# Layer one's last pair with seven partial second products, and some low parts on VectorE

## The chip, the cores and the metric

The kernel runs on one core of one Trainium2 chip. The metric is the device time of one execution in microseconds (us); the value before is 744.51, the median of three runs (744.11 to 745.92). The engines are TensorE (PE, with its weight loads PEld), VectorE (DVE), ScalarE (ACT), GpSimd (POOL) and SyncE (SP), which issues the transfers. Each engine does its own instructions in order.

## What is computed

An attention over clusters, whose result x has 1536 rows and 512 columns, is followed by two feed-forward layers. The change lies in the first of them and in the step to the second.

```python
x = attention(q, k, v, centroids)            # 1536 x 512
h = x @ moe_w_in                             # 512 -> 2048
x = np.maximum(0.01 * h, h) @ moe_w_out      # layer one
h = x @ moe2_w_in
r = np.maximum(h, 0.0)
return (r * r) @ moe2_w_out                  # layer two
```

All operands are float32. A float32 product is made of three matmuls in a shorter format: each operand is split into a high part (a cast) and a low part (operand minus its high part), and high by high, high by low and low by high are added up in PSUM.

## The kernel before

Layer m has the 1536 rows in three blocks b of 512 rows, and the 2048 inner columns in eight pairs f = 0, 2, ..., 14 of two 128-wide slices f and f + 1. For every pair the first product gives h, the activation gives g, and the second product adds to `acc[:, b, o]`, with o the four 128-column parts of the output. Blocks 0 and 1 of a pair form a two by two product. With seven first products in place of eight (Winograd's scheme), `quad` and `seven` compute P1 to P7; each is 2 x 3 matmuls of 512 columns. The inputs of these products are differences t1 to t4 of parts of x (`t_ops`; high parts `th`, low parts `tl`) and sums of the weights (`sum_pieces`, tile `ws`; block (m, f, 2)).

In layer one, pairs 4 to 12 (`SEVEN`) go through `seven`, which also does the second product of blocks 0 and 1 with seven products, M1 to M7, of six matmuls each, and needs one more sum of weights, block (0, f, 3), whose four additions GpSimd does in the pair before. Block 2 has plain products: u0 and u1 (12 matmuls each) and o0 to o3 (6 each). Such a pair has 132 matmuls. Pair 14, the last of layer one, goes through `step_list` and `quad`: eight second products, 138 matmuls, and block 2's second product at its very end.

The order on TensorE, VectorE, ScalarE and GpSimd is the program's own from pair 2 on (`manual_schedule`). Inside `seven` it is a string of names (`SEVEN_QUAD`): P1 is that product's matmuls, k1, k5 and k6 are ScalarE's copies of a bank to `q`, aV, aX and aW are VectorE's sums in the four banks U, V, W and X, B11 to B22 the activated blocks with h, f and l for the high part, the full value and the low part, T1 to T4 their differences, r1.0 the addition of a half of M1's bank to `acc`, f0 the same for o0. n0.2 is step 2 of block 0 of the pair after: step 0 loads the raw weights, 1 does the first arithmetic (ScalarE and GpSimd), 2 joins both halves (VectorE), 3 casts the high part `wh` (ScalarE), 4 subtracts the low part `wl` (GpSimd). c is the pair's own blocks (c3.1 is the high part of the sum block, c3.2 its low part) and l the pair after the next.

When the last addition of layer one to `acc` is made, `flush` also writes the next layer's x: high part `xh` by ScalarE, low part `xl`. For blocks 0 and 1 GpSimd does the low part, from `acc`; for block 2 VectorE adds into the PSUM bank itself and does the four low parts from that bank, after all four additions:

```python
x, eng = (ps, nc.vector) if b == 2 else (a, nc.gpsimd)
nc.vector.tensor_tensor(out=x, in0=ps, in1=a, op=ALU.add)
nc.scalar.copy(out=xh[:, o, c], in_=x)
```

Layer two's pair 0 is plain: units (0, 0), (0, 1) and (1, 0) of 12 matmuls, each followed by a maximum with zero on ScalarE, a square on VectorE, a cast to `gh` on ScalarE and a low part `gl` on VectorE; then the second product of unit (0, 0). The eight differences for layer two (`SUMS[1]`, L1285 in the rows) are GpSimd's, from `acc`.

Of the kernel before, what the change touches and what calls it, by code (L numbers as in the profile page):

```python
# [74 lines left out]
    "n1.2 g11 B22h B22f T3 T2 T1h T2h T1l T4 u0 T2l u0h u0f u0l T3h T3l n1.3 n1.4 "  # L75
) + SEVEN_REST + " h4.0 h4.1"
DOTS = {(0, 0): 0, (0, 1): 1, (1, 0): 2}


@with_exitstack  # L80
def attention_moe_moe_kernel(
# [25 lines left out]
    RING = 7  # L107
    SEVEN = (4, 6, 8, 10, 12)
    SIDE = 4
# [52 lines left out]
    def split_block(ci, t):  # L162
        pool = next(q for q, n in ring if ci % RING < n)
        wh = pool.tile([128, 2 * DM], F32R, tag="wh", name="wh")
        wl = pool.tile([128, 2 * DM], F32R, tag="wl", name="wl")
        weights[blocks[ci]] = (wh, wl)
        nc.scalar.copy(out=wh, in_=t)  # L167
        return lambda: nc.gpsimd.tensor_tensor(  # L168
            out=wl, in0=t, in1=wh.bitcast(F32), op=ALU.subtract
        )  # L170

    def decode_pieces(ci):
# [40 lines left out]

        def rest():
            st["rest"]()

# [10 lines left out]
    def sum_pieces(ci):  # L227

        st = {}
        K = DM // 2  # L230

        def sums():
            w = st["w"] = stg[1].tile([128, 4, K], F32, tag="ws", name="ws")
            m, f, j = blocks[ci]
            t0, t1 = (words[blocks.index((m, f, i))] for i in range(2))
            if j == 2:
                a11, a12, a21, a22 = t0[:, 0:K], t0[:, K : 2 * K], t1[:, 0:K], t1[:, K : 2 * K]
            else:
                a11, a12, a21, a22 = (
                    t[:, DM + i * K : DM + (i + 1) * K] for i in range(2) for t in (t0, t1)  # L240
                )
            for o, i, k, op in (
                (w[:, 0], a21, a22, ALU.add),
                (w[:, 1], w[:, 0], a11, ALU.subtract),
                (w[:, 2], a11, a21, ALU.subtract),
                (w[:, 3], a12, w[:, 1], ALU.subtract),
            ):
                nc.gpsimd.tensor_tensor(out=o, in0=i, in1=k, op=op)

        def high():  # L250
            st["rest"] = split_block(ci, st["w"].rearrange("p a b -> p (a b)"))

        return [sums, high, lambda: st["rest"]()]

# [766 lines left out]

    x_low = []

    def flush(m, b, g, o, ps, part=slice(0, 512)):
        a = acc[:, b, o, part]
        if g == 0:
            nc.scalar.copy(out=a, in_=ps)
            return
        if g < NF // 2 - 1:
            nc.vector.tensor_tensor(out=a, in0=ps, in1=a, op=ALU.add)  # L1030
            return
        if m == 0:
            c = slice(b * N, (b + 1) * N)
            x, eng = (ps, nc.vector) if b == 2 else (a, nc.gpsimd)
            nc.vector.tensor_tensor(out=x, in0=ps, in1=a, op=ALU.add)
            nc.scalar.copy(out=xh[:, o, c], in_=x)
            if b == 2:
                x_low.append((o, c, x))
                if o < 3:
                    return  # L1040
                todo = list(x_low)
                x_low.clear()
            else:
                todo = [(o, c, x)]
            for o, c, x in todo:
                eng.tensor_tensor(
                    out=xl[:, o, c], in0=x, in1=xh[:, o, c].bitcast(F32), op=ALU.subtract
                )
# [6 lines left out]
    def quad(m, f, behind=True):  # L1055
        f0, f1, s = ((m, f, j) for j in range(3))
# [10 lines left out]
        def first():  # L1067
            p(U, lambda k: w_in(f0, k), lambda k: x_in(k, 0), True)
            p1 = tmp()
            nc.scalar.copy(out=p1, in_=U)  # L1070
            p(V, lambda k: w_in(f0, 2 + k), lambda k: x_in(2 + k, 0), True)
            add(V, V, p1)
            if behind:
                act(m, 0, f, V)

        kept = []

        def second():
# [36 lines left out]
    def seven(f, prev, after, later):  # L1115
# [119 lines left out]
        for name, q, block, c, g, b, half in (  # L1235
# [19 lines left out]
        for o in range(4):  # L1255
            ops[f"o{o}"] = lambda o=o: last(o)
            ops[f"f{o}"] = lambda o=o: flush(0, 2, f // 2, o, st["o", o])
        for i, q in enumerate(prev):
            ops[f"bh{i}"] = lambda q=q: g2(*q)
        for c, base in (("n", after), ("l", later), ("c", (0, f))):  # L1260
            for k in range(4):
                for j in range(5):
                    ops[f"{c}{k}.{j}"] = lambda base=base, k=k, j=j: piece((*base, k), j)
        for kk in range(2):
# [68 lines left out]
    def step_list(m, f, prev):  # L1333
# [55 lines left out]

    def piece(block, j):  # L1390
# [5 lines left out]
        pieces[block][j]()  # L1396

# [11 lines left out]
    for m in range(2):  # L1409
        turn = 0  # L1410
        for f in range(0, NF, 2):
# [80 lines left out]
```

## Time and profile before

| what | us |
|---|---|
| median of three runs | 744.51 |
| the profiled execution, its own time | 747.96 |
| its span | 746.20 |
| TensorE busy | 738.1 |
| pair 12 of layer one, TensorE's first matmul to the next pair's first | 429.38 to 459.34 |
| pair 14 of layer one | 459.34 to 491.20 |

The profile is one execution. TensorE hardly stops from one end to the other, so a time is read as a number of matmuls and the waits between them. The other engines have room on average; what counts is which of their instructions TensorE waits for at one place. In a timeline each row has the start, the duration, the engine, the line and operation, and in brackets how long the engine stood still before and what it waited for.

### The profile page before, as it was taken

Reading aid. Unit: us, or ns where it says so; the run is one execution under the profiler, and the core shown is the slowest. Engines: PE = TensorE matmul, PEld = TensorE weight load, DVE = VectorE, ACT = ScalarE, POOL = GpSimd, SP = SyncE. Lnnn points to the kernel's source line nnn. Section 1 sums busy time; section 2 is a strip of 40 time slices with the busy share of each in tenths; the row PEclk is TensorE's granted clock in tenths of the full one; section 3 lists DMA queues with packets and bytes.
Section 4 is the critical chain, followed back from the end, with each engine's and each line's share of the span. In section 5 each row is a group of like instructions: output and inputs, shape, how many; then the busy total and the mean of one; then the engine's idle time right before and its main releaser. Section 6 shows DMA issues by size and latency. Waiting matters only on the chain.

```text
span 746.2 us, 11181 instructions
## 1 busy us (share of the span) xinstructions
PE 738.1 (99%) x4014; PEld 643.1 (86%) x4014; DVE 534.6 (72%) x845; ACT 453.2 (61%) x837; POOL 497.6 (67%) x467
## 2 busy tenths in 40 slices
PE   8999999999999999999999999999999999999998
PEld 7999999999998878888888888788888888888886
DVE  6989999999998535376766866564667666576655
ACT  5988988988999465356365463656644335443430
POOL 7999999999957747866797874599434342343400
PEclk8999999999999999999999999999999999999999
DMA  3494663662612311111121130211212111121004
GB/s 108 123 226 118 134 162 109 133 164 65 152 44 83 122 65 72 57 57 60 63 105 56 58 114 11 102 58 56 76 44 107 57 56 66 54 108 58 1 0 170
DMA packets 16407, 64.79 MB, mean 87 GB/s; under 512 B 3040, under 2 KB 4192, under 8 KB 11360
## 3 DMA queue, kind: packets, MB, share of 16 engines
q1 hardware_dynamic: 16352, 64.07, 28.9%
q8 instruction: 32, 0.52, 0.3%
q14 instruction: 23, 0.19, 0.1%
HBM read 43.02 MB, written 3.15 MB: 62 GB/s over the span
## 4 chain that ended last, share of the span: by engine, by line
PE 91%; ACT 3%; DVE 3%; POOL 2%; issue 1%; DMA 0%; POOLq 0%; DVEq 0%; ACTq 0%
PE h L910 32%; PE o L988 23%; PE A L576 8%; PE S L479 7%; PE T L541 7%; PE o L1217 6%; PE h L1217 4%; PE S L350 1%; ACT e L511 1%; DVE nm L501 1%; PE o L1018 1%; DVE el L558 1%; PE dots L350 1%; POOL xl L606 0%; POOL q L1285 0%
## 5 line engine op out<-in xcount | busy, mean ns | idle before, releaser
L168 POOL TENSOR_TENSOR wl<-wt,wh 128x1024 fp32r<-128x1024 f32 x32 | 77.3, 2416 | 74.4 <-ACT wh L167 73.9
L910 PE MATMUL h<-xh,wh 128*128 128x512 f32 x288 | 112.0, 391 | 0.3 <-DVE h L1063 0.3
L910 PE MATMUL h<-xh,wl 128*128 128x512 f32 x288 | 112.2, 389 | 0.0
L910 PE MATMUL h<-xl,wh 128*128 128x512 f32 x288 | 112.2, 389 | 0.0
L1030 DVE TENSOR_TENSOR acc<-o,acc 128x512 f32<-128x512 f32 x154 | 100.0, 685 | 11.8 <-PE o L988 11.8
L558 DVE TENSOR_TENSOR el<-T,eh 128x512 fp32r<-128x512 f32 x144 | 94.6, 683 | 2.9 <-ACT eh L552 2.2
L528 POOL TENSOR_SCALAR e<-e,r 128x768 f32<-128x768 f32 x96 | 86.4, 911 | 12.7 <-PE T L541 6.8
L501 DVE TENSOR_REDUCE nm<-S 128x1 f32<-128x768 f32 x96 | 90.9, 948 | 3.5 <-PE S L350 1.8
L511 ACT ACTIVATE e<-S,nm 128x768 f32<-128x768 f32 x96 | 87.2, 908 | 10.0 <-DVE ds L378 5.3
L479 PE MATMUL S<-hb 128*128 128x384 f32 x384 | 89.8, 348 | 0.3 <-ACT xt L589 0.2
L552 ACT CAST eh<-T 128x512 fp32r<-128x512 f32 x144 | 79.6, 590 | 8.7 <-PE T L541 8.5
L959 DVE TENSOR_TENSOR gl<-h,gh 128x512 fp32r<-128x512 f32 x66 | 45.0, 691 | 54.0 <-ACT h L954 35.6
L576 PE MATMUL A<-eh,vv 128*128 128x256 f32 x288 | 80.3, 308 | 0.6 <-DVE xt L598 0.6
L541 PE MATMUL T<-ident,e 128*128 128x128 f32 x576 | 79.7, 273 | 0.5 <-POOL e L528 0.5
L576 PE MATMUL A<-el,vv 128*128 128x256 f32 x288 | 73.0, 283 | 0.2 <-DVE el L558 0.2
L541 PEld LDWEIGHTS T<-ident,e 128*128 128x128 f32 x576 | 68.9, 143 | 3.6 <-POOL e L528 0.7
L988 PE MATMUL o<-wh,gh 128*128 128x512 f32 x184 | 71.6, 389 | 0.0
L988 PE MATMUL o<-wl,gh 128*128 128x512 f32 x184 | 71.6, 389 | 0.0
L988 PE MATMUL o<-wh,gl 128*128 128x512 f32 x184 | 71.6, 389 | 0.0
L944 ACT ACTIVATE t<-h 128x512 f32<-128x512 f32 x48 | 28.0, 599 | 71.3 <-PE h L910 38.0
L168 POOL TENSOR_TENSOR wl<-ws,wh 128x1024 fp32r<-128x1024 f32 x17 | 41.4, 2433 | 38.2 <-ACT wh L167 38.2
L910 PEld LDWEIGHTS h<-xh,wh 128*128 128x128 f32 x288 | 54.1, 188 | 12.4 <-DVE gl L1177 0.7
(188 smaller groups left out, 1750.0 us busy)
## 6 DMA issues: line engine op xcount, KB each, us to landing
wraw<-w SPq DMA_DIRECT2D x32, 1024.0 KB, 4.7
hb<-spl SPq DMA_DIRECT2D x14, 576.0 KB, 4.7
hb<-spl SPq DMA_DIRECT2D x42, 192.0 KB, 5.1
rqk<-qk SPq DMA_DIRECT2D x16, 384.0 KB, 3.8
rv<-v SPq DMA_DIRECT2D x8, 384.0 KB, 3.4
out<-q SPq DMA_DIRECT2D x11, 256.0 KB, 2.8
hb<-st SPq DMA_DIRECT2D x56, 24.0 KB, 1.9
out<-q SPq DMA_DIRECT2D x2, 128.0 KB, 1.8
```

Of the source, the lines that this page charges most:

```text
L168: return lambda: nc.gpsimd.tensor_tensor(out=wl, in0=t, in1=wh.bitcast(F32), op=ALU.subtract)
L479: nc.tensor.matmul(out=s[:, c, 0:HALF], lhsT=hb[:, a, i * 128 : (i + 1) * 128], rhs=hb[:, b, c * HALF : (c + 1) * HALF], start=(a == 0), s ...
L501: nc.vector.tensor_reduce(out=n, in_=s_t[t][:, :, 0:HALF], axis=AX.XY, op=ALU.max, negate=True)
L511: nc.scalar.activation(out=e.rearrange("p (a b) -> p a b", a=2), in_=s_t.pop(t)[:, :, 0:HALF], func=AF.Exp, bias=n_t.pop(t), scale=1.0, ac ...
L528: nc.gpsimd.tensor_scalar(out=e_t[t], in0=e_t[t], scalar1=r_t[t // 2][:, t % 2 : t % 2 + 1], scalar2=1.0, op0=ALU.mult, op1=ALU.mult,)
L541: nc.tensor.transpose(T[:, o : o + 128], e_t[2 * u + b][:, kc * 128 : (kc + 1) * 128], ident)
L552: nc.scalar.copy(out=eh[:, 2 * g : 2 * g + 2, :].rearrange("p a b -> p (a b)"), in_=T_t[u, g])
L558: nc.vector.tensor_tensor(out=el[:, 2 * g : 2 * g + 2, :].rearrange("p a b -> p (a b)"), in0=T_t.pop((u, g)), in1=eh[:, 2 * g : 2 * g + 2, ...
L576: nc.tensor.matmul(out=A, lhsT=w, rhs=m[:, kc, :], start=(kc == 0 and i == 0), stop=(kc == KC - 1 and i == 1),)
L910: nc.tensor.matmul(out=out, lhsT=l, rhs=r, start=(first and i == 0), stop=(i == n - 1), skip_group_check=not first,)
L988: nc.tensor.matmul(out=outs[o], lhsT=l, rhs=r, start=(first and i == 0), stop=(last and i == 2),)
L1030: nc.vector.tensor_tensor(out=a, in0=ps, in1=a, op=ALU.add)
```

## The change

Pair 14 also goes through `seven`, with an order of its own, `SEVEN_LAST`. Its four-fold sum of weights, block (0, 14, 3), is new work of GpSimd in pair 12. In that order a D at the end of a name puts a low part on VectorE: c3.2D and n0.4D (`wl`, 128 x 1024 each) and B11lD (128 x 512). `flush` now adds into `acc` for block 2 too, and the low parts of x for block 2 (x2.0 to x2.3) and for the last two column parts of block 0 (x0.2, x0.3) are kept for later and done by VectorE from `acc`. Six differences of layer two (t1, t2, t4) stand in the new order; before they were in `SUMS[1]` under -2 and -1.

```diff
+SEVEN_LAST = (
+    "n0.1 P1 k1 P2 c3.1 c3.2D n0.2 aV n1.0 P6 k6 B11h B11f P5 k5 B11lD n0.3 n0.4D P7 aX B22h B22f P3 "
+    "aW B12f P4 B21h B21f T1 T3 B21l T2 n1.1 T1h T2h T1l n1.2 T4 u0 T2l u0h u0f u0l T3h T3l n1.3 l0.0 "
+    "M1 M2 r1.0 r1.1 n1.4 r2.0 r2.1 B22l u1 u1h u1f u1l M6 M5 r6.0 r5.0 r5.1 r6.1 o0 f0 M3 T4h r3.0 M7 "
+    "r7.0 T4l r7.1 r3.1 o1 f1 M4 r4.0 r4.1 x0.2 x0.3 l0.1 t1.0 t1.1 t2.0 t2.1 t4.0 t4.1 o2 f2 o3 f3 "
+    "x2.0 x2.1 x2.2 x2.3 l0.2 l1.0"
+)
...
-    SEVEN = (4, 6, 8, 10, 12)
+    SEVEN = (4, 6, 8, 10, 12, 14)
...
-        return lambda: nc.gpsimd.tensor_tensor(
+        return lambda eng=nc.gpsimd: eng.tensor_tensor(
             out=wl, in0=t, in1=wh.bitcast(F32), op=ALU.subtract
         )
...
-            x, eng = (ps, nc.vector) if b == 2 else (a, nc.gpsimd)
-            nc.vector.tensor_tensor(out=x, in0=ps, in1=a, op=ALU.add)
-            nc.scalar.copy(out=xh[:, o, c], in_=x)
-            if b == 2:
-                x_low.append((o, c, x))
-                if o < 3:
-                    return
-                todo = list(x_low)
-                x_low.clear()
+            nc.vector.tensor_tensor(out=a, in0=ps, in1=a, op=ALU.add)
+            nc.scalar.copy(out=xh[:, o, c], in_=a)
+
+            def low(eng):
+                eng.tensor_tensor(
+                    out=xl[:, o, c], in0=a, in1=xh[:, o, c].bitcast(F32), op=ALU.subtract
+                )
+
+            if later is not None:
+                later[b, o] = low
             else:
-                todo = [(o, c, x)]
-            for o, c, x in todo:
-                eng.tensor_tensor(
-                    out=xl[:, o, c], in0=x, in1=xh[:, o, c].bitcast(F32), op=ALU.subtract
-                )
+                low(nc.gpsimd)
...
+            ops[n + "lD"] = lambda n=n: low(n, nc.vector)
...
-                ops[f"r{name}.{j}"] = lambda q=q, j=j, b=b, o=2 * half + j: flush(
-                    0, b, f // 2, o, st[q, j]
+                g = f // 2 if f < NF - 2 or name in "2347" else 1
+                ops[f"r{name}.{j}"] = lambda q=q, j=j, b=b, g=g, o=2 * half + j: flush(
+                    0, b, g, o, st[q, j], later=x_low if b == 0 and o > 1 else None
                 )
...
+            for b in (0, 2):
+                ops[f"x{b}.{o}"] = lambda b=b, o=o: x_low[b, o](nc.vector)
...
-        for name in (SEVEN_PLAIN if f < 2 * PLAIN[0] else SEVEN_QUAD).split():
+            for name in ("t1", "t2", "t4"):
+                ops[f"{name}.{kk}"] = t_by[1][kk][name]
+        order = SEVEN_PLAIN if f < 2 * PLAIN[0] else SEVEN_QUAD if f < NF - 2 else SEVEN_LAST
+        for name in order.split():
             ops[name]()
```

VectorE at the start of pair 14, before: after the last addition of pair 12 (`acc<-h`) come the sum in bank V (`h<-h,q`), the join of `wt`, and then low parts and sums.

```order
L1030 TENSOR_TENSOR acc<-h,acc 128x512
L1063 TENSOR_TENSOR h<-h,q 128x512
L206 SCALAR_TENSOR_TENSOR wt<-wt,wraw 128x1024
L959 TENSOR_TENSOR gl<-h,gh 128x512
L1063 TENSOR_TENSOR h<-h,q 128x512 x2
```

The same place now:

```order
L1035 TENSOR_TENSOR acc<-h,acc 128x512
L175 TENSOR_TENSOR wl<-ws,wh 128x1024
L213 SCALAR_TENSOR_TENSOR wt<-wt,wraw 128x1024
L1124 TENSOR_TENSOR h<-h,q 128x512
L1177 TENSOR_TENSOR gl<-t,gh 128x512
L175 TENSOR_TENSOR wl<-wt,wh 128x1024
L1124 TENSOR_TENSOR h<-h,q 128x512 x2
```

A low part of 128 x 1024 (c3.2D) and the join now stand ahead of the sum in V, and a second one (n0.4D) ahead of the sums in X and W.

VectorE at the step from layer one to layer two, before: the join for pair 2 of layer two, the four additions of block 2 and their low parts, and then the square and the low part of layer two's first unit.

```order
L206 SCALAR_TENSOR_TENSOR wt<-wt,wraw 128x1024
L1035 TENSOR_TENSOR o<-o,acc 128x512 x4
L1046 TENSOR_TENSOR xl<-o,xh 128x512 x4
L947 SCALAR_TENSOR_TENSOR h<-h,t 128x512
L959 TENSOR_TENSOR gl<-h,gh 128x512
```

The same place now, from the last additions of M4 (r4.0, r4.1) on:

```order
L1039 TENSOR_TENSOR acc<-o,acc 128x512 x2
L1043 TENSOR_TENSOR xl<-acc,xh 128x512 x2
L1039 TENSOR_TENSOR acc<-h,acc 128x512 x2
L1043 TENSOR_TENSOR xl<-acc,xh 128x512 x4
L213 SCALAR_TENSOR_TENSOR wt<-wt,wraw 128x1024
L954 SCALAR_TENSOR_TENSOR h<-h,t 128x512
L966 TENSOR_TENSOR gl<-h,gh 128x512
```

Six low parts that read `acc` and the join now stand ahead of the square; the four of before read a PSUM bank, and the join stood ahead of the additions.

GpSimd at the same step, now: the low part of layer two's second block, six low parts of x, the first step on the next raw weights, and the differences.

```order
L175 TENSOR_TENSOR wl<-wt,wh 128x1024
L1043 TENSOR_TENSOR xl<-acc,xh 128x512 x6
L207 TENSOR_SCALAR wraw<-wraw 128x1024
L1295 TENSOR_TENSOR q<-acc 128x512 x2
L1295 TENSOR_TENSOR q<-acc,q 128x512 x2
```

Before, it had eight low parts of x, four ahead of that block's low part and four behind the step on the raw weights, and then the same differences.

## Rows read from the trace of the kernel before

**Rows 1.** The page, part 1: busy us (share of the span) xinstructions.

```profile
PE 738.1 (99%) x4014; PEld 643.1 (86%) x4014; DVE 534.6 (72%) x845; ACT 453.2 (61%) x837; POOL 497.6 (67%) x467
```

**Rows 2.** Timeline of TensorE, pairs 12 and 14: start us, us, engine, what, [idle before].

```profile
429.38 0.39 PE L910 MATMUL h<-xh,wh 128*128 128x512 f32 x1
...
459.34 0.39 PE L910 MATMUL h<-xh,wh 128*128 128x512 f32 x1
...
467.28 0.39 PE L910 MATMUL h<-xh,wl 128*128 128x512 f32 x1
467.94 0.50 PE L910 MATMUL h<-xh,wh 128*128 128x512 f32 x1 [0.28 <-DVE h L1063]
...
491.20 0.39 PE L910 MATMUL h<-xh,wh 128*128 128x512 f32 x1
...
499.36 0.39 PE L988 MATMUL o<-wh,gh 128*128 128x512 f32 x1
```

**Rows 3.** Timeline of VectorE, first part of pair 12.

```profile
430.18 1.22 DVE L206 SCALAR_TENSOR_TENSOR wt<-wt,wraw 128x1024 int32<-128x1024 int32 x1
432.37 0.70 DVE L1124 TENSOR_TENSOR h<-h,q 128x512 f32<-128x512 f32 x1 [0.96 <-PE h L910]
436.43 0.70 DVE L1124 TENSOR_TENSOR h<-h,q 128x512 f32<-128x512 f32 x1 [3.37 <-PE h L910]
```

**Rows 4.** Timeline of GpSimd, the same place.

```profile
432.55 2.40 POOL L168 TENSOR_TENSOR wl<-ws,wh 128x1024 fp32r<-128x1024 f32 x1 [2.85 <-ACT wh L167]
```

**Rows 5.** Timeline of ScalarE, the same place.

```profile
431.42 1.05 ACT L167 CAST wh<-ws 128x1024 fp32r<-128x1024 f32 x1
...
434.14 0.60 ACT L1164 ACTIVATE gh<-h 128x512 fp32r<-128x512 f32 x1
...
435.11 0.61 ACT L1136 COPY q<-h 128x512 f32<-128x512 f32 x1
435.57 1.08 ACT L167 CAST wh<-wt 128x1024 fp32r<-128x1024 f32 x1
```

**Rows 6.** Timeline of VectorE and GpSimd, low parts (xl) with both inputs in SBUF.

```profile
340.27 1.29 DVE L1329 TENSOR_TENSOR xl<-t,xh 128x512 fp32r<-128x512 f32 x2
...
518.21 2.40 POOL L168 TENSOR_TENSOR wl<-wt,wh 128x1024 fp32r<-128x1024 f32 x1
...
519.39 1.77 DVE L1329 TENSOR_TENSOR xl<-t,xh 128x512 fp32r<-128x512 f32 x1 [0.78 <-ACT xh L1328]
...
520.57 2.85 POOL L168 TENSOR_TENSOR wl<-ws,wh 128x1024 fp32r<-128x1024 f32 x1
...
521.86 2.11 DVE L1329 TENSOR_TENSOR xl<-t,xh 128x512 fp32r<-128x512 f32 x1 [0.70 <-ACT xh L1328]
```

**Rows 7.** Timeline of VectorE and ScalarE, step to layer two.

```profile
492.00 2.48 DVE L1046 TENSOR_TENSOR xl<-o,xh 128x512 fp32r<-128x512 f32 x4
...
494.75 0.70 DVE L947 SCALAR_TENSOR_TENSOR h<-h,t 128x512 f32<-128x512 f32 x1 [0.26 <-ACT t L944]
...
495.48 0.59 ACT L956 CAST gh<-h 128x512 fp32r<-128x512 f32 x1 [0.77 <-DVE h L947]
```

**Rows 8.** Timeline of GpSimd, step to layer two.

```profile
493.03 2.54 POOL L1285 TENSOR_TENSOR q<-acc 128x512 f32<-128x512 f32 x2
```

**Rows 9.** Timeline of VectorE and GpSimd, around 256 us.

```profile
255.75 1.28 POOL L256 TENSOR_SCALAR xh<-xt 128x768 fp32r<-128x768 f32 x1
...
256.26 1.84 DVE L206 SCALAR_TENSOR_TENSOR wt<-wt,wraw 128x1024 int32<-128x1024 int32 x1
...
257.00 2.26 POOL L1285 TENSOR_TENSOR q<-q 128x512 f32<-128x512 f32 x1
```

**Rows 10.** Busy by stretch: PE PEld DVE ACT POOL busy (x), PEclk, DMA share, GB/s.

```profile
8.00:12.00 4.00, 4.00 (x22) 4.00 (x22) 2.71 (x6) 3.14 (x5) 3.04 (x2) 0.54 0.08 32
12.00:20.00 8.00, 8.00 (x52) 7.30 (x52) 5.69 (x12) 5.02 (x9) 4.75 (x4) 0.80 0.01 2
```

**Rows 11.** Waits of TensorE, the longest: us in total, times, longest.

```profile
PE ctp L312 <- DVE ct L310: 1.5, 1, 1.5
```

More of the change, by code (lines that the diff above doesn't have):

```diff
@@ L212, in high, with rest @@
             st["rest"] = split_block(ci, st["t"].bitcast(F32))
-        def rest():
-            st["rest"]()
+        def rest(*eng):
+            st["rest"](*eng)
         if ci < EARLY:
@@ L251, in high @@
             st["rest"] = split_block(ci, st["w"].rearrange("p a b -> p (a b)"))
-        return [sums, high, lambda: st["rest"]()]
+        return [sums, high, lambda *eng: st["rest"](*eng)]
     def pool_copy(out, in_):
@@ L1020, in last_rows, with flush @@
                 flush(1, b, NF // 2 - 1, o, ps, c)
-    x_low = []
-    def flush(m, b, g, o, ps, part=slice(0, 512)):
+    def flush(m, b, g, o, ps, part=slice(0, 512), later=None):
         a = acc[:, b, o, part]
@@ L1053, in flush, with quad @@
             nc.sync.dma_start(out=out[r : r + 128, part], in_=ob)
-    def quad(m, f, behind=True):
+    def quad(m, f):
         f0, f1, s = ((m, f, j) for j in range(3))
@@ L1072, in first @@
             add(V, V, p1)
-            if behind:
-                act(m, 0, f, V)
+            act(m, 0, f, V)
         kept = []
@@ L1082, in second @@
                 nc.scalar.copy(out=kept[-1], in_=q)
-            if not behind:
-                act(m, 0, f, V)
         def third():
@@ L1121, in seven @@
         ops = {}
+        x_low = {}
         def add(out, a, b, op=ALU.add):
@@ L1256, in seven @@
             ops[f"o{o}"] = lambda o=o: last(o)
-            ops[f"f{o}"] = lambda o=o: flush(0, 2, f // 2, o, st["o", o])
+            ops[f"f{o}"] = lambda o=o: flush(0, 2, f // 2, o, st["o", o], later=x_low)
+            for b in (0, 2):
+                ops[f"x{b}.{o}"] = lambda b=b, o=o: x_low[b, o](nc.vector)
         for i, q in enumerate(prev):
@@ L1263, in seven @@
                     ops[f"{c}{k}.{j}"] = lambda base=base, k=k, j=j: piece((*base, k), j)
+                    ops[f"{c}{k}.{j}D"] = lambda base=base, k=k, j=j: piece(
+                        (*base, k), j, nc.vector
+                    )
         for kk in range(2):
             ops[f"h4.{kk}"] = t_by[0][kk]["h4"]
-        for name in (SEVEN_PLAIN if f < 2 * PLAIN[0] else SEVEN_QUAD).split():
+            for name in ("t1", "t2", "t4"):
+                ops[f"{name}.{kk}"] = t_by[1][kk][name]
+        order = SEVEN_PLAIN if f < 2 * PLAIN[0] else SEVEN_QUAD if f < NF - 2 else SEVEN_LAST
+        for name in order.split():
             ops[name]()
@@ L1350, in step_list @@
             return seq, tail
-        first, second, third = quad(m, f, bool(behind))
-        behind = behind or [lambda: None] * 2
+        first, second, third = quad(m, f)
         seq = [
@@ L1358, in step_list @@
         if f == NF - 2:
-            if m == 1:
-                return seq + [lambda: last_rows(2)], []
-            return seq + [lambda: g2(*tail[0]), lambda: g2(*tail[1])], []
+            return seq + [lambda: last_rows(2)], []
         return seq, tail
@@ L1382, in attention_moe_moe_kernel @@
         {
-            -2: "t1.0 t1.1 t2.0 t2.1", -1: "t4.0 t4.1", 0: "t3.0 t3.1", 2: "h1.0 h1.1 l1.0 l1.1",
+            0: "t3.0 t3.1", 2: "h1.0 h1.1 l1.0 l1.1",
             3: "h2.0 h2.1", 4: "l2.0 l2.1", 5: "h3.0 l3.0", 6: "h3.1 l3.1", 8: "h4.0", 9: "h4.1",
@@ L1388, in attention_moe_moe_kernel, with piece @@
     pieces = {}
-    def piece(block, j):
+    def piece(block, j, *eng):
         if block not in blocks:
@@ L1395, in piece @@
             pieces[block] = (sum_pieces if block[2] > 1 else decode_pieces)(i)
-        pieces[block][j]()
+        pieces[block][j](*eng)
     def pair_after(m, f):
@@ L1435, in attention_moe_moe_kernel @@
                     piece((0, 2, 0), 0)
-                table = {(0, NF - 2): TURN_LAST, (1, 0): TURN_SEAM}.get((m, f), TURN)
+                table = TURN if (m, f) != (1, 0) else TURN_SEAM
                 for k, j in table[i] if i < len(table) else ():
@@ L1441, in attention_moe_moe_kernel @@
                 sums(m, turn)
-                if m == 0 and f == NF - 2:
-                    sums(1, i - len(seq))
                 turn += 1
```

3 lines of the change are left out of this document (removed).

## Prediction

> **What bounds the kernel now.** I read the page's busy shares first: TensorE is busy 99% of the span [rows 1]. So only two things can move the time: fewer matmuls, or a wait of TensorE. Next came TensorE's own timeline around the last pair of layer one [rows 2]. A 512-wide matmul starts every 0.2267 us (36 of them from 491.20 to 499.36: 8.16 / 36). The pair before the last, with 132 matmuls, runs from 429.38 to 459.34: 29.96 us against 132 x 0.2267 = 29.92. The last pair, with 138 matmuls in the plain order, runs from 459.34 to 491.20: 31.86 against 138 x 0.2267 = 31.28, so it loses 0.58; the largest piece is the gap in front of 467.94, where TensorE waits for VectorE (467.28 + 0.2267 = 467.51, so 0.43). Then I laid the other three engines beside it, since the change gives VectorE work that GpSimd had.
>
> **What the change takes away.** Six matmuls: 6 x 0.2267 = 1.36 us. With the new order the old gap has no place either, so the most that can be won is 31.86 - 29.92 = 1.94 us, 0.26% of 744.51. About 0.3% (2.2 us) is what a measurement of this kernel can tell from no change, so even the full gain would hardly show.
>
> **The start of the last pair.** I use the pair from 429.38 as the template, since the first seven products keep its order, and count from its first matmul as 0. P1, P2, P6, P5, P7, P3 and P4 then start at 0, 1.36, 2.72, 4.08, 5.44, 6.80 and 8.16. In the template VectorE does the join of wt at 0.80 and the sum aV at 2.99, as soon as P2 ends [rows 3], and the low part of the sum block (c3.2) runs on GpSimd for 2.40 [rows 4]. In the new order c3.2D stands on VectorE ahead of that join and of aV. It must wait for ScalarE's cast of the same block, 431.42 + 1.05, that is 3.09 [rows 5]. What a 128x1024 low part costs on VectorE no row shows. The nearest is the join, same size, two SBUF operands: 1.22 [rows 3]; GpSimd's 2.40 is the upper end, and twice the 0.65 of a 128x512 low part, 1.29, lies between [rows 6]. I take 1.22. In a row, an instruction starts about 0.1 before its predecessor's printed end (four low parts take 2.48, and a single 128x512 instruction 0.70 [rows 3, 7]). So: c3.2D at 3.15, the join at 4.28, aV at 5.41 to 6.11.
>
> ScalarE's queue stands behind aV: B11h, B11f, k5 and the cast n0.3 started at 4.76, 5.25, 5.73 and 6.19 [rows 5], and now B11h can't start before 6.15, which is 1.39 later; k5 ends at 7.73 and the cast at 8.66. P3 adds onto the bank that k5 copies, so it starts at 7.78 instead of 6.80: about 1.0 lost. On VectorE n0.4D needs that cast, so it runs from 8.72 to 9.94, and aX, queued behind it, from 9.85 to 10.55. P4 writes the bank that aX reads, so it starts at 10.60 instead of 8.16. **This term is +2.44** in all (the 1.0 is part of it). After P4 the queues stand as in the template and I carry them on by 2.44. Bounds: 0, if the work ahead of aX were hidden, as it is in the template, and 2.44 + 2 x (2.40 - 1.22) = 4.8 at GpSimd's price. GpSimd is idle in the template from 429.70 to 432.55 [rows 4], and in the new order it waits for the next raw weights after its first step, so I see nothing that slows c3.2D further. The new sum block for this pair (four GpSimd additions in the pair before) is what the earlier pairs also do without a gap; I cost it at nothing, with GpSimd's idle time as cover.
>
> Balance up to layer two's first matmul: 29.92 + 0.04 + 2.44 = 32.40 instead of 31.86, **+0.54**.
>
> **The seam.** Count now from layer two's first matmul, 0. M4 ends at -2.72 and o2, o3 fill the rest. Before, block 2's four low parts read PSUM (xl<-o) and took 2.48 together while GpSimd ran without a break [rows 7, 8]. The square of layer two's first unit then began at 494.75, 3.55 after 491.20, and TensorE needed its result only at 499.36, which is 8.16 [rows 2, 7]. In the new code these low parts, and the two of block 0, read acc and xh, both in SBUF, and GpSimd is busy there with four low parts of x, one step on raw weights and eight differences t.
>
> What two such streams do to each other the trace shows. With GpSimd idle, xl<-t,xh on VectorE takes 0.65 (two in 1.29). Beside a GpSimd low part that ran from 518.21 to 520.61 the same form started at 519.39 and took 1.77, that is until 0.55 after GpSimd ended; the next one, 2.11, ended 0.55 after the next GpSimd instruction, which itself took 2.85 instead of 2.40 [rows 6]. They exclude each other and take turns: at 256.26 a VectorE join was held until the GpSimd instruction of 255.75 had ended at 257.03, and the GpSimd one of 257.00 then took 2.26 instead of about 1.3 [rows 9]. The Trainium skill states it as a rule that speaks against this edit: SBUF — State Buffer, "Who interferes with whom", says that a VectorE instruction with two SBUF inputs and a GpSimd one that reads SBUF hold a shared read interface exclusively, and that one with at most one SBUF input doesn't contend. By that rule, the old form with its PSUM operand was safe and the new one isn't; the rows agree. The same notes also speak for the edit: GPSIMD Engine Reference, "Engine selection", puts elementwise work on VectorE because GpSimd is about twice as slow with two inputs (here 1.27 against 0.65). By that alone the sum would lose this whole term; that is the second rival.
>
> Turn by turn, GpSimd's steps at 1.27 [rows 8], the raw-weight step taken at the same 1.1 to 1.3, VectorE's at 0.60: GpSimd's last low part of x ends near -0.37 (four of them start when row block r3.0 is cast, about -5.45). x0.2 runs until 0.25, GpSimd until 1.4, x0.3 until 2.0. TensorE needs x0.3's result for its fourth slice at 2.04 + 0.23 = 2.27: just in time. f2 and f3 read PSUM and need no turn: 3.16. Then x2.0 to x2.3 each wait for one difference t: they end at 3.83, 5.70, 7.57 and 9.44. The join l0.2 also has two SBUF operands: from 10.7 to 11.86. Only then comes the square of layer two's first unit (0.70), gh on ScalarE until 13.15 and gl until 13.9. TensorE has three units of its own to do (36 matmuls, 8.16) and then waits for gh: 13.15 - 8.16 = 5.0, and 0.3 more for gl at its third matmul. **This term is +5.3.** Bounds: 0 with no turns lost (the square then begins at about 4.6 and gl ends near 6.7, under 8.16), and 5.3 + 1.3 if x0.3 comes one turn later. I take the upper chain since the rows with exactly this form show it. Later units of layer two follow at TensorE's pace, so I add nothing for them.
>
> **The sum.** -1.36 - 0.58 + 0.04 + 2.44 + 5.3 = +5.8. The profiled execution took 747.96 with a span of 746.20; it would take 753.8. The median of the runs is 744.51, 3.45 less, all of it outside this change: 744.51 + 5.8 = **750.3 us**.
>
> **Rivals.** (1) The seam doesn't bite: VectorE's queue gets through without giving GpSimd its turns, as four PSUM low parts did before [rows 7]. Only +0.54 is left: 745.0. Rows 6 and 9 speak against it; for it speaks that GpSimd could be further along than I put it. (2) Not slower: both covers hold and the six matmuls come out clean, as in the pairs before, -1.94: 742.6. Its place is aV: it decides from the point where c3.2D, the join and aV end before ScalarE would be free for B11h, 4.76 against my 6.11. That would need c3.2D to cost nothing, or aV to run ahead of it; the written order says otherwise. (3) Both stalls, and a lower clock after the long one: in the only slow stretch of the trace the granted clock was 0.54 over 4 us and 0.80 over the next 8 [rows 10]. With levels of 2.4 and 1.2 GHz that is 0.92 x 4 + 0.40 x 8 = 6.9 us at the lower one, so up to 3.4 us of work lost: 753.7. TensorE's longest wait in the whole trace is 1.5 us [rows 11], so nothing shows whether one of 5 us does this. (4) That the six matmuls don't go is no rival: the order of TensorE shows them gone.
>
> **How the numbers follow.** Forecast 0.53, rival 1 0.19, rival 2 0.11, rival 3 0.15, anything else 0.02. Predicted: 750.3. Range 744.8 to 753.8: it leaves out rival 2 and a little above rival 3. Slower by over 0.3% (above 746.7): forecast, rival 3 and a part of the rest, 0.69. Within: rival 1 and most of rival 2, 0.28. Faster by over 0.3% (below 742.3): 0.03. The forecast alone would be 748.8 to 751.8.
>
> **What would show it.** Right: TensorE waits for ScalarE's copy in front of P3 and for VectorE's sum in front of P4, 2.4 together; the VectorE low parts of x take 1.3 to 2 us instead of 0.65; TensorE stands for about 5 us in front of layer two's first second product. Wrong: aV right behind P2; low parts of 0.65 beside a busy GpSimd; or a pair of 29.9 us with no wait behind it. A granted clock under 1 after the seam would be rival 3.

## The result: 0.7% slower

| what | before | after |
|---|---|---|
| median (us), with the runs shown ahead | 745.92 (7 runs) | 750.48 (7 runs) |
| ratio after / before, 95% interval | | 1.0069 [1.0042, 1.0095] |
| profiled execution, its own time | 747.96 | 753.62 |
| its span | 746.20 | 751.8 |
| pair 14, TensorE's first matmul to layer two's first | 31.86 | 32.50 |
| layer two's first matmul to the end of the span | 255.00 | 260.66 |

One of the seven executions before took 813.53 us and stands apart, the others fall into two groups (744.06 to 745.92 and 747.34 to 749.16), and in the traces shown here that difference lies ahead of pair 14 (which starts between 455.35 and 460.27), so below I compare stretches of the traces, or the lowest times, when a median mixes both. The span grew by 5.6: 0.64 in pair 14, 5.66 behind it, and 0.70 less ahead of it (pair 14 starts at 458.64 instead of 459.34).

The page's first part, against [rows 1]: TensorE has six matmuls less and a busy share of 98% instead of 99%.

```profile
PE 737.7 (98%) x4008; PEld 641.1 (85%) x4008; DVE 548.4 (73%) x859; ACT 455.4 (61%) x841; POOL 502.1 (67%) x471
```

TensorE's longest waits (us in total, times, longest); before, the longest of all was 1.5 [rows 11]:

```profile
PE o L995 <- ACT gh L963: 3.7, 1, 3.7
PE ohT L742 <- DVE pads L728: 1.6, 1, 1.6
PE warm L298 <- POOL ident masks.py:199: 1.4, 1, 1.4
PE h L917 <- DVE h L1124: 1.2, 1, 1.2
PE h L917 <- ACT q L1136: 0.8, 1, 0.8
```

The first, fourth and fifth are new and are the three that the prediction named. The second isn't in the rows of before either; it lies near the program's start (the matmuls of `ohT` stand at 12 to 22 us), far ahead of the change, and not every trace has it: it is 1.6 again in the run with block 2's low parts from PSUM and 0.2 in the run with both cures. The places of the three in TensorE's timeline, against [rows 2] (start, us, [idle before]): P3 at 458.64 + 7.80, P4 at + 10.62, layer two's first matmul, and the first second product of layer two.

```profile
466.44 0.50 PE L917 MATMUL h<-xh,wh 128*128 128x512 f32 x1 [0.84 <-ACT q L1136]
...
469.26 0.50 PE L917 MATMUL h<-xh,wh 128*128 128x512 f32 x1 [1.15 <-DVE h L1124]
...
491.14 0.39 PE L917 MATMUL h<-xh,wh 128*128 128x512 f32 x1
...
499.08 0.39 PE L917 MATMUL h<-xh,wl 128*128 128x512 f32 x1
503.18 0.66 PE L995 MATMUL o<-wh,gh 128*128 128x512 f32 x1 [3.71 <-ACT gh L963]
503.63 0.63 PE L995 MATMUL o<-wl,gh 128*128 128x512 f32 x1
...
507.63 0.39 PE L917 MATMUL h<-xh,wh 128*128 128x512 f32 x1
```

After 499.08 the next matmul was due 0.2267 later, so TensorE stood for 503.18 - 499.30 = 3.88. Then most of them start 0.43 apart, not 0.2267: the first twelve take 4.45 (503.18 to 507.63) instead of 2.72, another 1.73 lost. The granted clock by stretch shows why (us, PE, PEld, DVE, ACT and POOL busy, PEclk, DMA share, GB/s):

```profile
499.30:503.20 3.90, 0.19 (x2) 0.03 (x1) 3.19 (x4) 0.66 (x2) 3.90 (x3) 1.00 0.14 29
503.20:508.00 4.80, 4.80 (x14) 3.64 (x15) 2.74 (x5) 3.17 (x6) 3.36 (x3) 0.64 0.53 200
508.00:512.00 4.00, 4.00 (x20) 3.27 (x19) 2.32 (x3) 3.47 (x6) 2.51 (x3) 1.00 0.16 33
```

Behind the long wait the granted clock is 0.64, which is mostly the 1.2 GHz level, and 1.00 (2.4 GHz) again after 508.

VectorE's timeline shows where both waits come from: first the start of pair 14, against [rows 3], then the seam, against [rows 7].

```profile
461.76 1.23 DVE L175 TENSOR_TENSOR wl<-ws,wh 128x1024 fp32r<-128x1024 f32 x1 [2.23 <-ACT wh L174]
462.90 1.22 DVE L213 SCALAR_TENSOR_TENSOR wt<-wt,wraw 128x1024 int32<-128x1024 int32 x1
464.04 0.69 DVE L1124 TENSOR_TENSOR h<-h,q 128x512 f32<-128x512 f32 x1
...
493.87 5.76 DVE L1043 TENSOR_TENSOR xl<-acc,xh 128x512 fp32r<-128x512 f32 x4
499.56 2.28 DVE L213 SCALAR_TENSOR_TENSOR wt<-wt,wraw 128x1024 int32<-128x1024 int32 x1
501.76 0.69 DVE L954 SCALAR_TENSOR_TENSOR h<-h,t 128x512 f32<-128x512 f32 x1
```

The sum aV, which stood at +2.99 in the template, runs at 464.04 - 458.64 = +5.40, behind c3.2D and the join. At the seam block 2's four low parts take 5.76 instead of 2.48, the join 2.28 where it takes 1.22 alone [rows 3], and the square of layer two's first unit starts at 501.76 - 491.14 = +10.62 instead of +3.55.

One low part and GpSimd's step beside it (GpSimd's differences took 2.54 for two before, [rows 8]) show the turns:

```profile
495.66 1.73 POOL L1295 TENSOR_TENSOR q<-acc,q 128x512 f32<-128x512 f32 x1
497.36 1.73 POOL L1295 TENSOR_TENSOR q<-acc,q 128x512 f32<-128x512 f32 x1
```

```profile
493.87 0.68 DVE L1043 TENSOR_TENSOR xl<-acc,xh 128x512 fp32r<-128x512 f32 x1
...
494.47 1.77 DVE L1043 TENSOR_TENSOR xl<-acc,xh 128x512 fp32r<-128x512 f32 x1
...
496.17 1.77 DVE L1043 TENSOR_TENSOR xl<-acc,xh 128x512 fp32r<-128x512 f32 x1
```

Each VectorE low part but the first lasts 1.77 (0.65 alone), and each GpSimd step 1.73 (1.27 alone): they go one by one, with a new low part every 1.70, so a VectorE instruction costs 1.12 more than alone, most of a GpSimd step.

### The profile page after: what moved, and what is told of

Read it like the earlier page. It is cut to its first block, busy times and chain, and to the rows that moved or that the text cites. A ratio compares the mean times of both kernels' runs of the same rounds, so it can differ in the third digit from the quotient of the medians.

```text
span 751.8 us, 11199 instructions
## 1 busy us (share of the span) xinstructions
PE 737.7 (98%) x4008; PEld 641.1 (85%) x4008; DVE 548.4 (73%) x859; ACT 455.4 (61%) x841; POOL 502.1 (67%) x471
## 4 chain that ended last, share of the span: by engine, by line
PE 87%; DVE 6%; ACT 4%; POOL 2%; issue 1%; DMA 0%; POOLq 0%; ACTq 0%; DVEq 0%
PE h L917 30%; PE o L995 21%; PE A L583 8%; PE S L486 7%; PE o L1218 7%; PE T L548 7%; PE h L1218 4%; PE S L357 1%; ACT e L518 1%; DVE xl L1043 1%; DVE nm L508 1%; PE o L1025 1%; DVE el L565 1%; POOL xl L613 0%; POOL q L1295 0%
## 5 line engine op out<-in xcount | busy, mean ns | idle before, releaser
L175 POOL TENSOR_TENSOR wl<-wt,wh 128x1024 fp32r<-128x1024 f32 x31 | 74.9, 2415 | 63.9 <-ACT wh L174 63.4
L1035 DVE TENSOR_TENSOR acc<-o,acc 128x512 f32<-128x512 f32 x160 | 103.7, 685 | 11.5 <-PE o L995 11.5
L966 DVE TENSOR_TENSOR gl<-h,gh 128x512 fp32r<-128x512 f32 x60 | 40.8, 690 | 44.7 <-ACT h L961 26.3
```

The source lines that it names most:

```text
L175: return lambda eng=nc.gpsimd: eng.tensor_tensor(out=wl, in0=t, in1=wh.bitcast(F32), op=ALU.subtract)
```

## Experiments

The theory has two separate losses: (A) at the start of pair 14 the two low parts of weights on VectorE delay aV and aX; (B) at the seam the low parts of x take turns with GpSimd because both operands lie in SBUF, the square comes late, TensorE stands, and its clock falls behind that. Rivals: one loss is only the other carried on; the place of the low parts rather than their operands delays the square; the low parts belong on GpSimd.

### The sum block's low part behind aV

```diff
-    "n0.1 P1 k1 P2 c3.1 c3.2D n0.2 aV n1.0 P6 k6 B11h B11f P5 k5 B11lD n0.3 n0.4D P7 aX B22h B22f P3 "
+    "n0.1 P1 k1 P2 c3.1 n0.2 aV c3.2D n1.0 P6 k6 B11h B11f P5 k5 B11lD n0.3 n0.4D P7 aX B22h B22f P3 "
```

> Only c3.2D, the 128x1024 low part on VectorE at the start of pair 14, moves from ahead of the join and aV to behind aV; the other one (n0.4D) stays ahead of aX. Theory (place in VectorE's queue, not the amount of its work, makes the wait): k5 is early again and TensorE doesn't wait in front of P3; n0.4D still waits for ScalarE's cast (end near 7.27 from the first matmul of the pair) and pushes aX to about 9.2, so TensorE waits about 1.0 in front of P4. The pair takes about 31.0 us in place of 32.5 and the time is about 749.0. Rival (VectorE's added work itself is what is late): the pair stays near 32.5, 750.5.

Measured: 749.95 us, ratio 1.0077 [1.0053, 1.0102]. The wait in front of P3 is gone, and pair 14 takes 31.82, 0.68 less than after; I had expected 31.0. The rest is lost in front of P4:

```profile
462.84 1.93 DVE L175 TENSOR_TENSOR wl<-wt,wh 128x1024 fp32r<-128x1024 f32 x1 [0.73 <-ACT wh L174]
464.70 1.28 DVE L1124 TENSOR_TENSOR h<-h,q 128x512 f32<-128x512 f32 x2
```

n0.4D takes 1.93 instead of 1.23: it meets GpSimd's step on the next raw weights (462.61, 1.09 long) and waits its turn. With c3.2D out of its way the join ends earlier (457.56, +2.03, instead of 464.12, +5.48), the load of those weights is issued right behind it, and so GpSimd's step comes at +7.08 instead of +10.39. So c3.2D's place costs the wait of P3, as worked out; what it gives back in front of P4 is cut by a turn that I had not seen coming.

### Both low parts out of the way of aV and aX

```diff
-    "n0.1 P1 k1 P2 c3.1 c3.2D n0.2 aV n1.0 P6 k6 B11h B11f P5 k5 B11lD n0.3 n0.4D P7 aX B22h B22f P3 "
+    "n0.1 P1 k1 P2 c3.1 n0.2 aV c3.2D n1.0 P6 k6 B11h B11f P5 k5 B11lD n0.3 n0.4 P7 aX B22h B22f P3 "
```

> As in e1, and the second 128x1024 low part (n0.4) goes back to GpSimd. Theory: no wait in front of P3 or P4, the pair takes 29.9 to 30.0 us, the time is 2.5 below the changed kernel, about 748.0; the wait at the first second product of layer two stays at 3.7 to 3.9. Rival (the two waits are separate causes and one lies elsewhere): one of the two waits stays, 749 to 750.

Measured: 748.72 us, ratio 1.0064 [1.0037, 1.0091]; the lowest time is 748.07 against 750.24 of after. Pair 14 takes 29.94, which is 132 matmuls and nothing else (its first matmul and layer two's first):

```profile
455.49 0.39 PE L917 MATMUL h<-xh,wh 128*128 128x512 f32 x1
...
485.43 0.39 PE L917 MATMUL h<-xh,wh 128*128 128x512 f32 x1
```

The seam is as it was (`o<-wh,gh` waits 3.72 for gh, granted clock 0.59 in the 4.2 us behind). So (A) is these two low parts and nothing more, and (B) does not come from (A). I call this edit the cleared start below.

### Block 2's low parts read PSUM

```diff
-    "r7.0 T4l r7.1 r3.1 o1 f1 M4 r4.0 r4.1 x0.2 x0.3 l0.1 t1.0 t1.1 t2.0 t2.1 t4.0 t4.1 o2 f2 o3 f3 "
-    "x2.0 x2.1 x2.2 x2.3 l0.2 l1.0"
+    "r7.0 T4l x2.0 r7.1 r3.1 o1 f1 M4 r4.0 r4.1 x0.2 x0.3 x2.1 l0.1 t1.0 t1.1 t2.0 t2.1 t4.0 t4.1 o2 f2 o3 f3 "
+    "x2.2 x2.3 l0.2 l1.0"
...
-            nc.vector.tensor_tensor(out=a, in0=ps, in1=a, op=ALU.add)
-            nc.scalar.copy(out=xh[:, o, c], in_=a)
+            x = ps if b == 2 else a
+            nc.vector.tensor_tensor(out=x, in0=ps, in1=a, op=ALU.add)
+            nc.scalar.copy(out=xh[:, o, c], in_=x)
...
-                    out=xl[:, o, c], in0=a, in1=xh[:, o, c].bitcast(F32), op=ALU.subtract
+                    out=xl[:, o, c], in0=x, in1=xh[:, o, c].bitcast(F32), op=ALU.subtract
...
-            ps = st["o", o] = bank((3, 2, 3, 2)[o])
+            ps = st["o", o] = bank(((3, 2, 3, 2) if f < NF - 2 else (3, 1, 3, 2))[o])
```

> The start of pair 14 as in the changed kernel. At the step to layer two the four low parts of block 2 stay on VectorE and ahead of the square, but read the PSUM bank instead of acc (x2.0 and x2.1 stand earlier since banks are used again, o1 takes bank V). Theory (turns with GpSimd over reads of SBUF): these four take 0.6 to 0.7 each, only x0.2, x0.3 and the join still take turns; the square starts near +7 instead of +10.6 from layer two's first matmul, the wait in front of the first second product is 0 to 0.9 and the clock stays at 1.00: 745.0 to 746.0. Rival (the length of VectorE's queue alone, six low parts and a join ahead of the square): the wait stays above 3 and the time near 750.

Measured: 744.93 us, ratio 1.0007 [0.9976, 1.0039]. VectorE at the seam:

```profile
488.73 2.85 DVE L1044 TENSOR_TENSOR xl<-acc,xh 128x512 fp32r<-128x512 f32 x2
491.51 0.68 DVE L1044 TENSOR_TENSOR xl<-h,xh 128x512 fp32r<-128x512 f32 x1
492.11 1.28 DVE L1040 TENSOR_TENSOR h<-h,acc 128x512 f32<-128x512 f32 x2
493.45 1.29 DVE L1044 TENSOR_TENSOR xl<-h,xh 128x512 fp32r<-128x512 f32 x2
494.65 1.67 DVE L213 SCALAR_TENSOR_TENSOR wt<-wt,wraw 128x1024 int32<-128x1024 int32 x1
496.25 0.69 DVE L954 SCALAR_TENSOR_TENSOR h<-h,t 128x512 f32<-128x512 f32 x1
```

Block 2's low parts take 0.68 for one and 1.29 for two, and GpSimd was busy beside them (`q<-acc` from 491.13, and more differences behind it); block 0's two, still from `acc`, take 2.85. The square starts at 496.25 - 489.86 = +6.39, TensorE goes on at +8.15 without a wait, and the granted clock stays at 1.00. The waits in front of P3 and P4 are those of after (0.84 and 1.16). So (B) goes as a whole, the lower clock with it, and it doesn't need (A).

### The same places, but still from SBUF

Only the order string of the run above, with its other three edits left out: x2.0 and x2.1 earlier, all four low parts from `acc`.

```diff
-    "r7.0 T4l r7.1 r3.1 o1 f1 M4 r4.0 r4.1 x0.2 x0.3 l0.1 t1.0 t1.1 t2.0 t2.1 t4.0 t4.1 o2 f2 o3 f3 "
-    "x2.0 x2.1 x2.2 x2.3 l0.2 l1.0"
+    "r7.0 T4l x2.0 r7.1 r3.1 o1 f1 M4 r4.0 r4.1 x0.2 x0.3 x2.1 l0.1 t1.0 t1.1 t2.0 t2.1 t4.0 t4.1 o2 f2 o3 f3 "
+    "x2.2 x2.3 l0.2 l1.0"
```

> Only the places of two of block 2's low parts change (x2.0 behind T4l, x2.1 behind x0.3, as in the run with PSUM operands); all four still read acc in SBUF. It tells the place from the operand. Theory (the SBUF operand and the turns it takes with GpSimd): the low parts of block 2 take 1.3 to 1.8 us each beside a busy GpSimd, layer two's first square begins 9 to 10.5 us after layer two's first matmul, TensorE waits 2 to 4 us for gh, and the time is 748 to 750. Rival (their place behind o3 and f3 is what delayed the square): the square at about +6.4, no wait, and about 744.9, as in that run.

Measured: 750.67 us, ratio 1.0071 [1.0048, 1.0095], above the expected 748 to 750. Part of that lies in pair 14, which takes 33.04 instead of 32.50: in its earlier place x2.0 waits for GpSimd as well (1.06 long), the addition behind it comes later, and a matmul that waits for that addition starts 0.40 late. VectorE at the seam:

```profile
487.46 4.55 DVE L1043 TENSOR_TENSOR xl<-acc,xh 128x512 fp32r<-128x512 f32 x3
491.94 1.28 DVE L1039 TENSOR_TENSOR acc<-h,acc 128x512 f32<-128x512 f32 x2
493.30 3.37 DVE L1043 TENSOR_TENSOR xl<-acc,xh 128x512 fp32r<-128x512 f32 x2
496.60 2.28 DVE L213 SCALAR_TENSOR_TENSOR wt<-wt,wraw 128x1024 int32<-128x1024 int32 x1
498.80 0.69 DVE L954 SCALAR_TENSOR_TENSOR h<-h,t 128x512 f32<-128x512 f32 x1
```

The square is back at 498.80 - 488.57 = +10.23, and TensorE stands for 3.48 in front of 500.21. The operand decides, not the place: x2.2 and x2.3 at the same spot take 3.37 from `acc` and 1.29 from PSUM. (The two runs also differ in the bank of o1, which the PSUM form needs.) By the Trainium skill (SBUF — State Buffer, "Who interferes with whom") a VectorE instruction with two SBUF inputs contends with GpSimd's reads and one with at most one doesn't; these two runs agree, 3.37 against 1.29.

### The join behind the first unit

The join l0.2 and the load l1.0 leave the pair's order and go behind the low part of layer two's first unit.

```diff
-    "x2.0 x2.1 x2.2 x2.3 l0.2 l1.0"
+    "x2.0 x2.1 x2.2 x2.3"
...
-        (), ((0, 3),), ((1, 1),), ((0, 4), (1, 2)), (), ((2, 0), (3, 0)),
+        ((0, 2), (1, 0)), ((0, 3),), ((1, 1),), ((0, 4), (1, 2)), (), ((2, 0), (3, 0)),
```

> Only the join l0.2 and the load behind it move from ahead of the square of layer two's first unit to behind its low part. Theory: the square starts one turn earlier, 2.2, so TensorE's wait shrinks from 3.9 to about 1.7. If the lower clock comes from the length of that wait, it stays at 1.00 and the time falls by 3.9, to about 746.6; if the clock falls whatever the length, by 2.2, to about 748.3. Rival (VectorE's queue isn't what is late, but ScalarE's or GpSimd's): no change, 750.5.

Measured: 749.57 us, ratio 1.0079 [1.0049, 1.0110]; neither expected time. The granted clock stays at 1.00, but other waits are there:

```profile
PE o L995 <- ACT gh L963: 1.5, 1, 1.5
PE warm L298 <- POOL ident masks.py:199: 1.4, 1, 1.4
PE o L995 <- ACT acc L1032: 1.2, 1, 1.2
PE h L917 <- DVE h L1124: 1.2, 1, 1.2
PE h L917 <- POOL wl L175: 0.8, 1, 0.8
```

The seam's loss of 3.88 + 1.73 shrinks to a stand of 1.67 and 0.40 in the twelve matmuls behind it. The 1.2 and the 0.8 are new: they cost 1.61 + 1.23 - 2 x 0.23 = 2.38 by the starts of the matmuls. The load behind the join is issued at 504.78, +12.0 from layer two's first matmul instead of +10.8, so the weights of the next block arrive later. ScalarE's `wt<-wraw` waits 0.94 for that transfer; behind it in ScalarE's queue stand four casts, then the step t that the next square waits 1.24 for, the cast of that square's result and the copy to `acc` that TensorE waits for. The stand and the clock went as the theory says; I had left out the load. That the load alone makes the new waits is read from this chain, and no run with the join moved and the load left in its place shows it apart.

### All low parts on GpSimd

```diff
-    "n0.1 P1 k1 P2 c3.1 c3.2D n0.2 aV n1.0 P6 k6 B11h B11f P5 k5 B11lD n0.3 n0.4D P7 aX B22h B22f P3 "
+    "n0.1 P1 k1 P2 c3.1 c3.2 n0.2 aV n1.0 P6 k6 B11h B11f P5 k5 B11l n0.3 n0.4 P7 aX B22h B22f P3 "
...
-                ops[f"x{b}.{o}"] = lambda b=b, o=o: x_low[b, o](nc.vector)
+                ops[f"x{b}.{o}"] = lambda b=b, o=o: x_low[b, o](nc.gpsimd)
```

> Seven second products in pair 14, with every low part that the change gave to VectorE back on GpSimd, at the same places of the order (c3.2, B11l, n0.4, x0.2, x0.3, x2.0 to x2.3). Theory (VectorE's queue at both places is the whole loss): the start is that of the earlier pairs, no wait; at the step to layer two GpSimd does x0.2 and x0.3 right behind its four low parts of x and is done with x0.3 at about 2.2 from layer two's first matmul, where TensorE needs it at 2.27, so a wait of 0 to 0.3; the square comes on time and the clock stays at 1.00. Time about 1.6 to 1.9 below the kernel before, 742.0 to 742.4. Rival (GpSimd is the engine that must be relieved): x0.3 or the differences come too late on GpSimd, a wait of over 1 us appears in layer two's first unit or in its pair 2, and the time is that of before or above.

Measured: 749.24 us, ratio 1.0063 [1.0045, 1.0081]: a miss by 7 us. Block 2's four low parts had not come from GpSimd: in the kernel before they were VectorE's, from PSUM, so this run and the next two put them on GpSimd for the first time. Pair 14 is clean (29.97), but the wait has only moved: in front of the third of layer two's second products, at 509.09, TensorE stands for 4.6, and the granted clock is 0.54 in the 5.3 us behind. VectorE's join l1.2 waits 9.37 for GpSimd's step on the raw weights here. The next run, with the cleared start, asks the same of block 2's four low parts alone.

### Block 2's low parts on GpSimd, ahead of the raw weights

```diff
-                ops[f"x{b}.{o}"] = lambda b=b, o=o: x_low[b, o](nc.vector)
+                ops[f"x{b}.{o}"] = lambda b=b, o=o: x_low[b, o](nc.vector if b == 0 else nc.gpsimd)
```

> The start of e2 (c3.2D behind aV, n0.4 on GpSimd) and block 2's four low parts on GpSimd, behind the six differences; x0.2 and x0.3 stay on VectorE. Theory: no wait in pair 14 (29.9 to 30.0 us), the square near +6 from layer two's first matmul, no wait in front of the first second product, clock 1.00: 1.9 below the kernel before, about 742.0. Rival (the step to layer two needs these low parts early, or GpSimd's longer queue delays layer two's pair 2): a wait of over 1 us later, 743 to 744.

Measured: 747.47 us, ratio 1.0051 [1.0033, 1.0068]: a miss again, with the same kind of wait. GpSimd, and then VectorE:

```profile
495.36 5.06 POOL L1043 TENSOR_TENSOR xl<-acc,xh 128x512 fp32r<-128x512 f32 x4
500.37 2.55 POOL L1295 TENSOR_TENSOR q<-acc 128x512 f32<-128x512 f32 x2
503.00 1.10 POOL L207 TENSOR_SCALAR wraw<-wraw 128x1024 int32<-128x1024 uint32 x1
```

```profile
504.13 1.23 DVE L213 SCALAR_TENSOR_TENSOR wt<-wt,wraw 128x1024 int32<-128x1024 int32 x1 [7.73 <-POOL wraw L207]
505.27 0.69 DVE L954 SCALAR_TENSOR_TENSOR h<-h,t 128x512 f32<-128x512 f32 x1
```

The four low parts stand ahead of GpSimd's step on the raw weights, VectorE's join l1.2 waits 7.73 for that step, and the square queued behind the join comes late, with ScalarE's cast of its result and the copy to `acc` behind that: TensorE waits for that copy and stands for 2.8 in front of the third second product, and the granted clock is 0.61 in the 4.4 us behind. That pointed to the place of the four low parts in GpSimd's queue.

### Block 2's low parts on GpSimd, behind the raw weights

The cleared start again; x2.0 to x2.3 leave the pair's order, and `late` keeps them until layer two's step on the raw weights has been issued.

```diff
-        x_low = {}
+        x_low = late
...
+    late = {}
...
+                if (m, f, i) == (1, 0, 2):
+                    for o in range(4):
+                        late[2, o](nc.gpsimd)
```

> The cleared start of pair 14, and block 2's four low parts x2.0 to x2.3 on GpSimd as in the kernel before, but behind the raw-weight step of the join l1.2 instead of ahead of it. Theory (what decides is the place of GpSimd's low parts: in the run with x2.0 to x2.3 ahead of the raw step the join l1.2 was 7.7 us late): the join l1.2 is on time, no wait of TensorE of over 0.5 us at the first two of layer two's second products, granted clock 1.00 there, pair 14 at 29.9 us, and the time 1.5 to 1.9 us below the kernel before (about 742.4). Rival (GpSimd's amount of work is too great wherever it stands): a wait of 1 to 3 us in front of a unit of block 2, whose low parts then come late, and a time of 743 to 746.

Measured: 750.76 us (747.52 to 754.0), ratio 1.0069 [1.0042, 1.0095]. TensorE's longest waits:

```profile
PE h L916 <- POOL wl L174: 2.5, 1, 2.5
PE warm L297 <- POOL ident masks.py:199: 1.4, 1, 1.4
PE h L916 <- POOL xl L1042: 0.7, 3, 0.3
PE o L994 <- ACT acc L1031: 0.7, 1, 0.7
```

The theory of the place falls. (The expectation's "as in the kernel before" isn't so: there these four were VectorE's.) The third of layer two's second products, where the run before stood, has no wait now, and the granted clock is 1.00, but unit (2, 0) waits three times for the low parts, and then a low part of the weights, queued behind them, is 2.5 late. From layer two's first matmul to the end it takes 746.0 - 485.67 = 260.3 instead of 255.0. In both places that I tried, four more low parts (5 us) on GpSimd make something late. That the amount decides is the nearest reading: here GpSimd never stands still for more than 0.1 from 480.16 to 525.17. It is not shown, since other places weren't tried.

### The two cures together

The cleared start and block 2's low parts from PSUM, both diffs as above.

> The start of e2 and the PSUM low parts of e3 together. Theory: the two losses are separate and both go; 0.3 lost at most at the step. Time 1.5 to 1.9 below the kernel before, 742.0 to 742.4, which is 2.5 below e3. Rival (they overlap, so that one hides the other): less than 1.5 below e3.

Measured: 742.66 us (742.23 to 742.76 in seven runs, 745.59 to 747.64 in five), before 744.01, ratio 0.9996 [0.9976, 1.0016]. The times can't be told from those of before by that interval; the lowest are 742.23 against 743.77. The trace says the same as these:

```profile
455.41 0.39 PE L917 MATMUL h<-xh,wh 128*128 128x512 f32 x1
...
485.57 0.39 PE L917 MATMUL h<-xh,wh 128*128 128x512 f32 x1
```

Pair 14 takes 30.16 (31.86 before), layer two to the end 255.0 (255.0), and no wait of TensorE is longer than the 1.4 at the program's start. That is 1.7 less, of the 1.94 that the prediction had as the most to be won. By the lowest times it is 2.5 below the run with the PSUM low parts alone (744.74), as expected of two losses that are separate.

## Why the prediction was right, and where only its sum was

**Six matmuls and the old gap, -1.94.** Shown: with both low parts out of the way, pair 14 takes 29.94, against the 29.92 of 132 matmuls.

**The start of the pair, +2.44.** P3 came at 7.80 (worked out: 7.78), P4 at 10.62 (10.60), and the 128x1024 low part took 1.23 where I took the join's 1.22 from bounds of 1.22 and 2.40. Pair 14 took 32.50 for 32.40. The cause is shown by the run that clears both. What I didn't see is that n0.4D is not safe from a turn with GpSimd either (1.93 in the first experiment); in the changed kernel that step of GpSimd came only at 469.03, when its transfer had landed, and n0.4D had ended by 468.60.

**The seam, +5.3.** 3.88 + 1.73 = 5.61 were lost. The mechanism is shown (3.37 against 1.29 for the same two low parts, by their operand), but the sum came out near by luck, with two errors against each other. The stand itself was 3.88, not the 5.0 worked out. The term that was too large is the chain of turns: x0.3 ended at +1.6 instead of +2.0 and x2.0 at +3.41 instead of +3.83; the three low parts behind it took 1.70 each from end to end where I had 0.60 + 1.27 = 1.87; and the join ended 2.21 behind them instead of 2.42. So it ended at +10.70 instead of +11.86, and TensorE went on at +12.04 instead of +13.15. And the forecast had no price for the clock: rival 3's mechanism happened, at 1.73 instead of up to 3.4. By the sign that the prediction named for it, a granted clock under 1 behind the seam, what ran is rival 3, which had 0.15; only the number is the forecast's. The forecast and rival 3 weren't alternatives as I had set them; the right case was the forecast's wait, shorter, with rival 3's clock behind it. The 0.3 that I added for gl can't be seen apart here, since the third matmul started in the slower stretch.

**From the profiled execution to the median.** 747.96 + 5.8 = 753.8 for a span like that of before, and the profiled execution took 753.62. The lowest times are 750.24 and 744.06, 6.18 apart, near the 0.64 + 5.66 of the traces. The medians of seven runs are 4.56 apart, because that of before had moved to 745.92; I had started from 744.51, the median of its first three runs. So 750.3 against 750.48 is a closer hit than the working of +5.8 deserves.

**The rivals.** Rival 1 (VectorE doesn't give turns) is refuted by the 1.77 of the low parts. (The prediction calls the loss of the whole seam term its second rival; by its own list, with +0.54 left, that is the first.) Rival 2 (both covers hold) decides at 4.76 against 6.11 for the end of aV; it ended at 464.04 + 0.69 - 458.64 = 6.09. A rule of the Trainium skill that spoke for the edit (GPSIMD Engine Reference, "Engine selection": elementwise work on VectorE) is half of what the runs show: in the two places tried GpSimd couldn't take block 2's four low parts without a wait of TensorE (747.47 and 750.76), and VectorE could only with an operand in PSUM (744.93 against 750.67).

## What to carry to other kernels

Before work moves from GpSimd to VectorE, or an operand of VectorE's from PSUM to SBUF, look at where the operands lie and what GpSimd does meanwhile: with both in SBUF, a low part took 1.77 instead of 0.65, and the next join in the queue 2.28 instead of 1.22; with one operand kept in PSUM block 2's four low parts cost nothing at the seam. Read the order of an in-order engine for what stands ahead of the one result that TensorE needs next; here two low parts of 1.2 us, put ahead of sums, cost 2.5 together, and with one behind its sum and the other back on GpSimd nothing. When a stall is priced, add what the clock may take behind it, and when a step is moved, move its load in the sum too.

## What the runs showed of the hardware

TensorE's granted clock fell with the longer stands and not with the shorter ones. After stands of 3.88 (the changed kernel), 4.6 and 2.8 (low parts on GpSimd) the granted clock was 0.64, 0.54 and 0.61 over the next 4.8, 5.3 and 4.4 us. It was 1.00 behind a stand of 2.64 (low parts behind the raw weights) and in the run with the join moved, whose stand was 1.67:

```profile
502.60:506.00 3.40, 3.39 (x14) 2.51 (x15) 2.75 (x4) 1.10 (x3) 3.40 (x3) 1.00 0.20 31
```

What such a fall costs is not set by the length of the stand alone: behind the same 3.88 the first twelve matmuls took 4.45 in the changed kernel, 4.66 with the start cleared and 5.28 with only the sum block's low part moved, instead of 2.72. That the stand causes the fall is not shown apart: no run kept the stand and took away something else. What the runs do show is that the lower clock was gone wherever the stand was gone or short, and that the transfers in the slow stretch (DMA share 0.53) do not lower it by themselves: in the run with the PSUM low parts the share was 0.61 at the same place (498 to 502), with a granted clock of 1.00.

And VectorE and GpSimd take strict turns when both have instructions queued that read SBUF (two inputs there on VectorE's side): at the seam of the changed kernel neither got two in a row from 494.47 to the end of the join. A pair of one low part and one step of GpSimd takes 1.70, a little less than the sum of both alone (0.65 + 1.27 = 1.92).
